# RetNet attention and a tanh-shrink feed-forward layer in one kernel: two thirds of the k and q transposes done by a DMA of 16-bit halves

**Chip, cores, metric.** One core of a Trainium2 chip. The metric is the device time of one execution in microseconds, the median of several. SBUF and PSUM are the core's on-chip memories (every tile here has up to 128 rows, called partitions), HBM is the memory outside the core.

## What the kernel computes

A recurrent attention block and, on its output, a feed-forward layer. All in float32.

```python
# attention: q, k, v of shape (4, 8, 768, 64), a state of 64x64 for each head
for t in range(S):
    state = gamma * state + k[:, :, t] (outer product) v[:, :, t]
    y[:, :, t] = scale * q[:, :, t] @ state
x = y.transpose(0, 2, 1, 3).reshape(B * S, H * D)      # 3072 x 512
# feed-forward: w_in 512 x 2048, w_out 2048 x 512
h = x @ w_in
out = (h - tanh(h)) @ w_out
```

## The kernel before

The kernel takes the sequence in 24 chunks of 128 tokens. A chunk's attention is a handful of small products on TensorE, in which k and q stand on the partitions by head dimension. So each chunk needs k and q transposed: four 128x128 blocks each. TensorE does it by matmuls with the identity, and ScalarE copies the result out of PSUM.

```python
def turn(ci, which, early=False):
    ...                                   # a pair of PSUM banks
    t = loaded[ci][which]
    for p in range(NP):                   # NP = 4 pairs of heads
        nc.tensor.transpose(tp[:, ts(p, P)],
                            t[:, ds(2 * p, 2)].rearrange("p h d -> p (h d)"), ident)

def turn_chunk(ci):
    if ci < NCH:
        turn(ci, 0)                       # k
        turn(ci, 1)                       # q
        turn_copy(ci)                     # one ScalarE copy, PSUM -> kqT in SBUF
```

Around the attention runs the feed-forward layer, as 96 steps. A step is an up projection (16 matmuls into h), the non-linearity (five activations on ScalarE, six operations on VectorE), and the down projection of two steps earlier (8 matmuls into o). The first 8 steps and the chunks 0 to 7 are ordered by hand. After that a loop feeds one chunk into every second step, and steps 8 to 26 also convert weight tiles, on ScalarE, VectorE and GpSimd (a cut; the conditions at both ends of the range are left out):

```python
with_chunk = {BEGUN + 2 * i + 1: FIRST - 3 + i for i in range(NCH - FIRST + 3)}   # 8, 8
for i in range(14, NW):
    with_weights[i - 5] = [i]

for s in range(BEGUN, len(steps)):
    ci = with_chunk.get(s)
    if ci is not None:
        scale(ci + 3, ...)                # GpSimd: q and v by powers of gamma
        outputs_rest(ci); keep_x(ci)
        products(ci + 2); mask(ci + 2); state(ci + 2)     # these need kqT of ci + 2
        load_chunk(ci + 4)
        outputs(ci + 1); see(ci + 1)
    for i in with_weights.get(s, []):
        convert(i); load_weights(i + 3)
    up(...); shrink(...)                  # (four calls)
    downs(LAG)                            # down of step s - 2; stores of results
    if ci is not None:
        turn_chunk(ci + 3)
```

All DMAs but one are issued on SyncE, whose queue is in program order: an entry that waits holds up those behind it.

## Time and profile before

| | before |
|---|---|
| median of 4 runs | 767.60 us (767.25 to 767.75) |
| span of the profiled run | 766.0 us |
| TensorE (PE) busy | 754.9 us, 99% |
| VectorE (DVE) busy | 524.5 us, 68% |
| ScalarE (ACT) busy | 375.3 us, 49% |
| DMA, mean of the span | 56 GB/s |

The lines on which the argument stands are shown in the prediction.

### The profile page before, as it was taken

Reading aid. Unit: us, or ns where it says so; the run is one execution under the profiler, and the core shown is the slowest. Engines: PE = TensorE matmul, PEld = TensorE weight load, DVE = VectorE, ACT = ScalarE, POOL = GpSimd, SP = SyncE. Lnnn points to the kernel's source line nnn. Section 1 sums busy time; section 2 is a strip of 40 time slices with the busy share of each in tenths; the row PEclk is TensorE's granted clock in tenths of the full one; section 3 lists DMA queues with packets and bytes.
Section 4 is the critical chain, followed back from the end, with each engine's and each line's share of the span. In section 5 each row is a group of like instructions: output and inputs, shape, how many; then the busy total and the mean of one; then the engine's idle time right before and its main releaser. Section 6 shows DMA issues by size and latency. Waiting matters only on the chain.

```text
span 766.0 us, 13968 instructions
## 1 busy us (share of the span) xinstructions
PE 754.9 (99%) x5598; PEld 517.1 (68%) x5598; DVE 524.5 (68%) x807; ACT 375.3 (49%) x709; POOL 124.3 (16%) x108
## 2 busy tenths in 40 slices
PE   8899999999999999999999999999999999999997
PEld 7776666677677667766766666666666666666663
DVE  4999899898898666556555665666655665666653
ACT  3666576565656444454443444434443444434442
POOL 0564444543443311110000000000000000000000
PEclk9999999999999999999999999999999999999999
DMA  9972444445441223320000000000000000000000
GB/s 204 225 188 57 125 111 111 124 115 121 113 110 43 69 70 77 97 50 2 15 15 1 14 15 0 29 0 1 27 1 1 27 1 0 29 0 1 27 1 27
DMA packets 89808, 42.99 MB, mean 56 GB/s; under 512 B 76304, under 2 KB 84624, under 8 KB 89744
## 3 DMA queue, kind: packets, MB, share of 16 engines
q1 hardware_dynamic: 89600, 41.95, 22.0%
q8 instruction: 44, 0.72, 0.4%
q10 hardware_dynamic: 144, 0.15, 0.1%
q14 instruction: 20, 0.16, 0.1%
HBM read 35.80 MB, written 6.29 MB: 55 GB/s over the span
## 4 chain that ended last, share of the span: by engine, by line
PE 95%; DVE 2%; SPq 1%; DMA 1%; ACT 0%; issue 0%; DVEq 0%
PE h L402 43%; PE o L450 42%; PE y L340 3%; PE kqTp L248 3%; PE s L286 1%; PE s L292 1%; SPq L227 1%; DMA raw<-in_moe_w_in_dram 1%; PE kqTp L210 0%; DVE head L183 0%; SPq L152 0%; DVE head L181 0%; PE y L210 0%; DVE power L185 0%; DVE head L179 0%
## 5 line engine op out<-in xcount | busy, mean ns | idle before, releaser
L402 PE MATMUL h<-xT,w 128*128 128x256 f32 x1536 | 349.9, 381 | 0.0
L450 PE MATMUL o<-w,g 128*128 128x512 f32 x768 | 345.5, 593 | 0.5 <-DVE g L441 0.5
L402 PEld LDWEIGHTS h<-xT,w 128*128 128x128 f32 x1536 | 288.5, 190 | 62.9 <-issue 26.5
L450 PEld LDWEIGHTS o<-w,g 128*128 128x128 f32 x768 | 145.5, 190 | 144.4 <-issue 136.3
L411 ACT ACTIVATE u<-h 128x512 f32<-128x512 f32 x96 | 57.3, 597 | 297.9 <-PE h L402 297.9
L427 DVE TENSOR_TENSOR th<-h,th 128x512 f32<-128x512 f32 x96 | 66.3, 691 | 183.9 <-ACT th L412 183.4
L441 DVE COPY_PREDICATED g<-large,th 128x512 f32<-128x512 int32 x96 | 75.4, 785 | 10.9 <-DVE g L440 1.4
L430 DVE SCALAR_TENSOR_TENSOR h<-q,h 128x512 f32<-128x512 f32 x96 | 66.9, 697 | 10.0
L436 DVE SCALAR_TENSOR_TENSOR h<-q,h 128x512 f32<-128x512 f32 x96 | 66.8, 696 | 9.9
L419 ACT ACTIVATE q<-u,tab 128x512 f32<-128x512 f32 x96 | 69.4, 723 | 0.0
L420 ACT ACTIVATE q<-u,tab 128x512 f32<-128x512 f32 x96 | 69.1, 720 | 0.0
L421 ACT ACTIVATE large<-u,tab 128x512 f32<-128x512 f32 x96 | 68.8, 717 | 0.0
L440 DVE TENSOR_TENSOR g<-h,u 128x512 f32<-128x512 f32 x96 | 66.3, 691 | 3.3
L428 DVE SCALAR_TENSOR_TENSOR h<-u,h 128x512 f32<-128x512 f32 x96 | 65.8, 685 | 0.0
L412 ACT ACTIVATE th<-h 128x512 f32<-128x512 f32 x96 | 56.8, 592 | 0.0
L193 POOL TENSOR_TENSOR low<-low,power 128x512 f32<-128x512 f32 x30 | 38.6, 1286 | 110.6 <-DVE power L185 55.0
L234 POOL TENSOR_TENSOR q<-q,tab 128x512 f32<-128x512 f32 x22 | 23.6, 1072 | 107.6 <-DMA q<-in_q_dram 101.9
L197 POOL TENSOR_TENSOR w<-low,head 128x512 f32<-128x512 f32 x30 | 38.5, 1283 | 2.4
L260 ACT COPY kqT<-kqTp 128x1024 f32<-128x1024 f32 x20 | 20.2, 1012 | 22.6 <-PE kqTp L248 22.4
L340 PEld LDWEIGHTS y<-a,v 64*64 64x64 f32 x768 | 16.1, 136 | 15.0 <-ACT large L421 11.4
L234 POOL TENSOR_TENSOR v<-v,tab 128x512 f32<-128x512 f32 x22 | 24.9, 1131 | 0.8 <-DMA v<-in_v_dram 0.8
L370 ACT COPY seen<-y 64x1 f32<-64x1 f32 x96 | 10.1, 154 | 24.8 <-PE y L340 24.4
(47 smaller groups left out, 398.1 us busy)
## 6 DMA issues: line engine op xcount, KB each, us to landing
k<-in_k_dram SPq DMA_DIRECT2D x24, 256.0 KB, 4.5
q<-in_q_dram SPq DMA_DIRECT2D x24, 256.0 KB, 5.0
v<-in_v_dram SPq DMA_DIRECT2D x24, 256.0 KB, 5.3
raw<-in_moe_w_out_dram SPq DMA_DIRECT2D x12, 512.0 KB, 3.5
out_dram<-sum SPq DMA_DIRECT2D x24, 256.0 KB, 2.0
raw<-in_moe_w_in_dram SPq DMA_DIRECT2D x14, 256.0 KB, 3.0
raw<-in_moe_w_in_dram SPq DMA_DIRECT2D x28, 128.0 KB, 3.5
raws<-in_moe_w_out_dram SPq DMA_DIRECT2D x4, 512.0 KB, 5.7
```

Of the source, the lines that this page charges most:

```text
L402: nc.tensor.matmul(hp, w1[:, c, ts(2 * m2 + i, P)], xT[n // 2][:, c, ts(n % 2, TH)], start=(i == 0 and c == 0), stop=(c == NC - 1), skip_g ...
L411: nc.scalar.activation(u, hp, AF.Square)
L419: nc.scalar.activation(q0, u, AF.Square, bias=bias0)
L420: nc.scalar.activation(q1, u, AF.Square, bias=bias1, scale=math.sqrt(A))
L421: nc.scalar.activation(large, u, AF.Relu, bias=bias_m)
L427: nc.vector.tensor_tensor(th, hp, th, op=ALU.subtract)
L428: nc.vector.scalar_tensor_tensor(hp, in0=u, scalar=R, in1=hp, op0=ALU.subtract, op1=ALU.mult, reverse0=True)
L430: nc.vector.scalar_tensor_tensor(hp, in0=q0, scalar=C0, in1=hp, op0=ALU.add, op1=ALU.mult)
L436: nc.vector.scalar_tensor_tensor(hp, in0=q1, scalar=A * C1, in1=hp, op0=ALU.add, op1=ALU.mult)
L440: nc.vector.tensor_tensor(flat, hp, u, op=ALU.mult)
L441: nc.vector.copy_predicated(flat, large.bitcast(I32), th)
L450: nc.tensor.matmul(o_p[j], gT[n, m2][:, i, ts(j, P)], w2[:, 2 * m2 + i], start=(first and i == 0), stop=(last and i == 1))
```

## The change

Its intent is to take the transposes of chunks 8 to 23 off TensorE. The transposing DMA is given 2-byte elements here (why is said in the prediction). So ScalarE separates the low and high 16 bits of k and q, a DMA stores the halves to a scratch in HBM as rows "token, half", and a transposing DMA loads them so that the two halves of a word lie side by side again in SBUF. As this way is long, a chunk comes in every third step only. Two small parts of the diff, a name for the 16-bit type and a default for a `pop`, are left out below.

```diff
+    dram = ctx.enter_context(tc.tile_pool(name="dram", bufs=2, space=bass.MemoryType.DRAM))
-    def turn_chunk(ci):
-        if ci < NCH:
-            turn(ci, 0)
-            turn(ci, 1)
-            turn_copy(ci)
+    def turn_by_dma(ci):
+        apart = mid.tile([P, 2, 2, H * D], U16, tag="apart", name=f"apart_{ci}", bufs=1)
+        for which in range(2):
+            words = loaded[ci][which].rearrange("p h d -> p (h d)").bitcast(U16)
+            nc.scalar.copy(out=apart[:, :, which],
+                           in_=words.rearrange("p (n two) -> p two n", two=2))
+        rows = dram.tile([P, 2, 2 * H * D], U16, tag="rows", name=f"rows_{ci}")
+        nc.sync.dma_start(out=rows, in_=apart.rearrange("p two i n -> p two (i n)"))
+        sides[ci] = mid.tile([P, 2, NP, P], F32, tag="kqT", name=f"kqT_{ci}")
+        nc.sync.dma_start_transpose(
+            out=sides[ci].rearrange("p i n t -> p (i n) t").bitcast(U16),
+            in_=rows.rearrange("p two n -> (p two) n"),
+        )
...
-    with_chunk = {BEGUN + 2 * i + 1: FIRST - 3 + i for i in range(NCH - FIRST + 3)}
+    with_chunk = {BEGUN + 3 * i + 1: FIRST - 3 + i for i in range(NCH - FIRST + 3)}
...
-        if ci is not None:
-            turn_chunk(ci + 3)
+        if ci is not None and ci + 3 < NCH:
+            turn_by_dma(ci + 3)
```

More of the change, by code (lines that the diff above doesn't have):

```diff
@@ L12 @@
 U32 = mybir.dt.uint32
+U16 = mybir.dt.uint16
 AF = mybir.ActivationFunctionType
@@ L327, in outputs @@
         vh = loaded[ci][2]
-        turned.pop(ci)
+        turned.pop(ci, None)
         qT = sides.pop(ci)[:, 1]
```

## The prediction

> **What bounds the kernel now.** I read the page from its first part to its fourth, and then the chain in order of time.
>
> ```profile
> span 766.0 us, 13968 instructions
> PE 754.9 (99%) x5598; PEld 517.1 (68%) x5598; DVE 524.5 (68%) x807; ACT 375.3 (49%) x709; POOL 124.3 (16%) x108
> PE 95%; DVE 2%; SPq 1%; DMA 1%; ACT 0%; issue 0%; DVEq 0%
> ```
>
> TensorE is busy for 99% of the span at a granted clock of 0.998, and 95% of the chain that ended last runs on it. A busy PE alone would not prove a bound. The chain in order of time does: it is the answer on one pair of steps, in which a chunk of the attention is fed into the stream of feed-forward tiles.
>
> ```profile
> 337.12 0.39 PE y L340 x16
> 337.52 0.47 PE s L286 x32
> 337.98 0.47 PE s L292 x32
> 338.45 0.70 PE y L340 x36
> 339.15 3.65 PE h L402 x16
> 342.80 3.43 PE o L450 x8
> 346.23 0.87 PE kqTp L248 x8
> 347.11 3.46 PE h L402 x16
> 350.56 1.72 PE o L450 x4
> ```
>
> The reader is to see that each piece begins where the one above it ended, and that the whole pair is on PE. The eight transposes of a chunk (kqTp) sit in this chain with 0.87 us. The last piece is cut by the window; the table of a wider window has it as 3.43 us. So a chunk costs PE 0.39 + 0.47 + 0.47 + 0.70 = 2.03 us for its products, 0.87 us for its transposes, and 3.65 - 3.46 = 0.19 us in the up projection after the products. A plain step is 3.46 + 3.43 = 6.89 us. The pair is 2.03 + 3.65 + 3.43 + 0.87 + 3.46 + 3.43 = 16.87 us, which is also the distance to the next pair in the trace. Nothing in it is a wait.
>
> **What the groups say of the operations concerned.** By form:
>
> ```profile
> L248 PE MATMUL kqTp<-tab,k 128*128 128x128 f32 x96 | 15.5, 287 | 0.3 <-DMA k<-in_k_dram 0.2
> L248 PE MATMUL kqTp<-tab,q 128*128 128x128 f32 x96 | 14.5, 274 | 0.0
> L260 ACT COPY kqT<-kqTp 128x1024 f32<-128x1024 f32 x20 | 20.2, 1012 | 22.6 <-PE kqTp L248 22.4
> L411 ACT ACTIVATE u<-h 128x512 f32<-128x512 f32 x96 | 57.3, 597 | 297.9 <-PE h L402 297.9
> L419 ACT ACTIVATE q<-u,tab 128x512 f32<-128x512 f32 x96 | 69.4, 723 | 0.0
> ```
>
> A transpose lasts some 280 ns by itself, but eight overlap to 0.87 us, that is 0.109 us each. The chain's number must be used: eight times the mean would give 2.2 us, and those are not to be had. ScalarE sits idle for 297.9 us waiting for PE, so it has room.
>
> **What the Trainium skill says.** Three places bear on this.
>
> "TensorE: Matmul & The Clock Gate", Part 4: PE-mode transpose: about 275 ns in a kernel's context, with the output in PSUM, so that a copy must follow. The trace agrees: 274 and 287 ns, and the copy is the group of 1012 ns.
>
> "DMA: Bandwidth & Descriptors", DMA Transpose (X-bar): only 2-byte elements, only into SBUF. Hence the halves: ACT splits low and high words, and their transposes interleave again into 32-bit words. The same page, Latency and other measured facts, gives the DMA transpose 261 GB/s in one kernel. No run before has one, so the trace cannot confirm it.
>
> "VectorE: DVE Perf Modes", The three transpose paths: 1309 ns for one 128x128 block of 16-bit elements by DMA. The trace is silent on this too. A chunk has 2 (k, q) x 4 x 2 (halves) = 16 such blocks. Whether they run side by side or in a row is the main uncertainty here.
>
> **The change part by part.**
>
> Removed from PE: the transposes of chunks 8 to 23, 16 chunks of 0.873 us (from pairs of this chain with 0.87 and 0.88) = 14.0 us. They are all on the path. The up projection after them takes 3.46 us, as it does after a down projection, so no further gain hides there. The PSUM pair used for them becomes free, but no PE wait was for it in the steady part.
>
> Moved: a chunk comes every three steps instead of two. Its work is the same. The last one comes at step 8 + 3*18 + 1 = 63 instead of 45. Tile column n=11, which needs chunks 22 and 23, begins at step 88, and n=4, which needs chunks 8 and 9, begins at step 32 and gets the latter at step 21. So the slower pace costs nothing by itself, and the new period is 16.87 - 0.87 + 6.89 = 22.89 us.
>
> Added on ScalarE: two copies of 1024 elements of a partition each, SBUF to SBUF, in place of one from PSUM. A 512-wide operation takes 0.72 us from SBUF (L419) and 0.60 from PSUM (L411), so I estimate 1.01 + 0.12 = 1.13 us each, 2.26 us for a chunk. That is 1.25 us more, 20 us in all, beside PE.
>
> Added on the queues: a store of 512 KB to HBM, a wait on the same queue until it has landed, and a transposing load of 512 KB. What landing takes today:
>
> ```profile
> k<-in_k_dram SPq DMA_DIRECT2D x24, 256.0 KB, 4.5
> v<-in_v_dram SPq DMA_DIRECT2D x24, 256.0 KB, 5.3
> raw<-in_moe_w_out_dram SPq DMA_DIRECT2D x12, 512.0 KB, 3.5
> out_dram<-sum SPq DMA_DIRECT2D x24, 256.0 KB, 2.0
> ```
>
> The store lies between the 2.0 us of half as much and the 3.5 us of a load of the same size; I take 3.0, and 0.2 for the issue.
>
> Is it in time? I measure from the beginning of a chunk's step (337.12 in the chain). These rows of ScalarE's timeline show the moment at which it is free:
>
> ```profile
> 345.03 0.71 ACT L421 ACTIVATE large<-u,tab 128x512 f32<-128x512 f32 x1
> 347.14 1.01 ACT L260 COPY kqT<-kqTp 128x1024 f32<-128x1024 f32 x1 [1.40 <-PE kqTp L248]
> ```
>
> At 345.74, so 8.62 us in, the step's activations end, and the new copies can begin at once (q was scaled by GpSimd long before, since its chunk was loaded a period earlier). Copies end at 8.62 + 2.26 = 10.88; the store has landed at 10.88 + 3.2 = 14.1. The products that need the result begin one period later, after the products of k and v: 22.89 + (337.98 - 337.12) = 23.75. The transposing load may therefore take 23.75 - 14.1 = 9.6 us from issue to landing before PE waits at all.
>
> What will it take? 512 KB at the skill's 261 GB/s is 2.0 us, and some 2 to 3 us go to issue and receipt, as for the other transfers, so 4 to 5 us. The loads of k, q and v support this: they move 768 KB in 256-byte pieces and all have landed some 6.5 us after the first issue (two issues of about 0.5 us, then 5.3). My estimate is 5 us (4 to 7), which leaves 4 to 5 us to spare. Sum: 767.5 - 14.0 = 753.5 us. I add 0.7 us for occasional late weights or stores on the same in-order queue: **754.2 us**, a gain of 1.7%.
>
> **The rivals.**
>
> A: a wait takes the place of the work. If the 16 blocks run one after the other, the load takes 16 x 1.309 = 20.9 us, PE waits 20.9 - 9.6 = 11.3 us for each chunk, and the time is 753.5 + 16 x 11.3 = 934 us. A milder form, 12 us to landing, gives 2.4 us each and 792 us. For it: the number in the skill, and that the pace was slowed to three steps, which says that the way through HBM is long. Against it: other transfers of this shape spread over all 16 engines. At two steps the room would be 9.6 - 6.9 = 2.7 us, too little even for my 5 us, so the third step is explained without this rival.
>
> B: the issuing queue becomes the bound. SyncE now stands still until the store has landed, and weights and stores of results queue behind it. For it: until about step 28 it carries a weight tile a step. Against it: the weights are asked for three steps ahead, and the stall is some 3 us in 22.9. I expect 0 to 3 us in all, or 754 to 757.
>
> C: ScalarE delays the stream. It has 2.26 us more after the activations, and the next step's h is ready only at 9.11 + 3.46 = 12.57 us, against copies that end at 10.88. It stays hidden; if the halves were twice as slow as estimated (4.5 us, ending at 13.1), the next activations slip by half a microsecond, which the lag of two tiles absorbs. 753.5.
>
> D: more gain than counted. It would need over 15.4 us from PE to pass 2%, and only 14.0 are there.
>
> **Range and chances.** The mechanism without waits ends between 752 and 757 us; I give that some 70%. Some 10% go to small waits, up to 775. The rest, 20%, is a transposing load that is well over its 9.6 us, with no natural upper end. So the range is 751.5 to 775. To be over 2% faster, the time must be under 752.2, which the sum barely forbids: 5%. To be over 2% slower it must be over 782.9, rival A: 18%. Within 2%: 77%.
>
> **What would show each step right or wrong.** Right: the L248 groups fall from 96 to 32 each, the chain in order of time holds products, up, down, up, down, up, down without a gap in 22.89 us, PE busy falls by some 14 us, the two ACT copies take about 1.1 us, and the issue table shows the store at about 3 and the transposing load at 4 to 7 us. Wrong: a wait of PE or PEld at the products (s) for a DMA into kqT, or a landing time above 9.6 us; then rival A holds, and the time lost should be 16 times the excess. Waits of the weight conversion for its DMA would be rival B, and PE waits for ACT or DVE in a chunk's steps rival C.

## More of the kernel before

One more view is of use later: the busy share in 40 equal slices of the span (19 us each; 9 is 90% or more).

```profile
PE   8899999999999999999999999999999999999997
DVE  4999899898898666556555665666655665666653
```

PE is full from the third slice on. DVE, whose mean is 68%, is nearly full up to the thirteenth slice, some 250 us: this is where the weights are converted. A mean over the span hides that.

## The result

| | before | after |
|---|---|---|
| median | 767.60 us | 754.76 us (754.43 to 754.93, 4 runs) |
| span of the profiled run | 766.0 us | 752.6 us |
| PE busy | 754.9 us | 739.6 us |
| ACT busy | 375.3 us | 389.1 us |
| DMA, mean | 56 GB/s | 79 GB/s |

The ratio is 0.9833 (95% interval 0.9816 to 0.985), that is 12.8 us or 1.7% faster. Ratios here are the mean time of one kernel's fast runs over that of the other's of the same rounds, so not quite the ratio of the medians quoted.

From the page of the changed kernel, the span, the engines, and the two new kinds of transfer with their median time to landing:

```profile
span 752.6 us, 13801 instructions
PE 739.6 (98%) x5470; PEld 501.9 (67%) x5470; DVE 518.7 (69%) x807; ACT 389.1 (52%) x725; POOL 125.9 (17%) x108
rows<-apart SPq DMA_DIRECT2D x16, 512.0 KB, 2.6
kqT<-rows SPq DMA_TRANSPOSE x16, 4.3
```

PE has 5470 matmuls in place of 5598: 128 less, 16 chunks of 8. Its busy time fell by 15.3 us where 14 were forecast; 1.1 of these lie in the first 97 us (90.81 against 89.75), before the loop. The store lands in 2.6 us (predicted 3.0), the transposing load in 4.3 us (predicted 5). The groups by form (line, engine, operation, shapes, count | busy us, mean ns | idle before):

```profile
L250 PE MATMUL kqTp<-tab,k 128*128 128x128 f32 x32 | 5.1, 282 | 0.4 <-DMA k<-in_k_dram 0.3
L250 PE MATMUL kqTp<-tab,q 128*128 128x128 f32 x32 | 5.0, 278 | 0.2 <-DVE q L236 0.2
L273 ACT COPY apart<-q 128x1024 uint16<-128x1024 uint16 x16 | 16.8, 1048 | 0.0
L273 ACT COPY apart<-k 128x1024 uint16<-128x1024 uint16 x16 | 16.6, 1036 | 0.0
```

Transposes on PE fell from 96 to 32 of each kind. The two copies of 16-bit words take 1.04 us each (estimated 1.13). The chain that ended last, in order of time, over one period:

```profile
353.48 0.39 PE y L352 x16
353.87 0.47 PE s L298 x32
354.34 0.47 PE s L304 x32
354.81 0.70 PE y L352 x47
355.51 3.65 PE h L414 x16
359.16 3.43 PE o L462 x8
362.59 3.45 PE h L414 x16
...
372.93 3.43 PE o L462 x8
376.37 0.39 PE y L352 x16
```

There is no gap: the period is 376.37 - 353.48 = 22.89 us, as worked out ahead. The products that read kqT (s L304) begin as soon as those before them end, so the load is in time.

Where did the 14.0 us go that the transposes had taken? I compared the start of the first up matmul of each step in the two traces. At step 9, before the first chunk of the loop, the changed kernel is 0.50 us ahead (104.11 against 104.60), from the hand-ordered beginning, whose waits made it end up to 1.3 us earlier or later in the traces taken here. At step 64, after the last chunk, it is 13.39 us ahead. So the loop won 12.9 us, 1.1 less than 14.0. The loss is at one place. Step 15 begins 9.89 us after step 14 where 8.77 are usual, since PE waited for DVE (timeline of the changed kernel, rows of DVE and PE):

```profile
142.95 0.73 DVE L453 COPY_PREDICATED g<-large,th 128x512 f32<-128x512 int32 x1
143.57 1.28 DVE L471 TENSOR_TENSOR sum<-o,sum 128x512 f32<-128x512 f32 x2
...
144.30 1.12 PE L462 MATMUL o<-w,g 128*128 128x512 f32 x2 [0.86 <-DVE sum L471]
```

The down projection needs a PSUM bank that DVE has yet to add to the running sum. DVE runs without a pause there (from 118 to 147 us in its timeline).

### The profile page after: what moved, and what is told of

Its sections match the earlier page's. It is cut to its first block, busy times and chain, and to the rows that moved or that the text cites. A ratio compares the mean times of both kernels' runs of the same rounds, so it can differ in the third digit from the quotient of the medians.

```text
span 752.6 us, 13801 instructions
## 1 busy us (share of the span) xinstructions
PE 739.6 (98%) x5470; PEld 501.9 (67%) x5470; DVE 518.7 (69%) x807; ACT 389.1 (52%) x725; POOL 125.9 (17%) x108
## 4 chain that ended last, share of the span: by engine, by line
PE 94%; DVE 2%; DMA 1%; SPq 1%; ACT 1%; issue 1%; DVEq 0%; ACTq 0%
PE h L414 43%; PE o L462 43%; PE y L352 3%; PE s L298 2%; PE s L304 1%; DMA raws<-in_moe_w_in_dram 1%; PE kqTp L250 1%; DMA k<-in_k_dram 1%; SPq L229 1%; PE kqTp L212 0%; DVE head L185 0%; PE y L212 0%; SPq L154 0%; DVE head L183 0%; DVE g L453 0%
## 5 line engine op out<-in xcount | busy, mean ns | idle before, releaser
L453 DVE COPY_PREDICATED g<-large,th 128x512 f32<-128x512 int32 x96 | 72.1, 751 | 10.6 <-ACT apart L273 0.5
L236 POOL TENSOR_TENSOR v<-v,tab 128x512 f32<-128x512 f32 x22 | 26.5, 1206 | 0.2 <-DMA v<-in_v_dram 0.2
L352 PE MATMUL y<-a,v 64*64 64x64 f32 x768 | 21.1, 224 | 2.3 <-issue 1.8
```

The costliest lines, as they stand in the source:

```text
L352: nc.tensor.matmul(y[ds(D * col, D), r, p // 2, ts(a, D)], lhsT, rhs, start=start, stop=True, skip_group_check=True)
L453: nc.vector.copy_predicated(flat, large.bitcast(I32), th)
```

## The experiments

My theory: the gain is TensorE's time for the 128 transposes and nothing else; the way through HBM is free because it has time to spare; the missing 1.1 us is DVE's backlog. The rivals: that the slower pace, or the freed PSUM banks and ScalarE's copy, made part of the gain; that the load only just comes in time; that something other than DVE ate the 1.1 us.

### The pace alone (e1), and both ways at once (e6)

```diff
 e1, on the kernel before:
-    with_chunk = {BEGUN + 2 * i + 1: ...
+    with_chunk = {BEGUN + 3 * i + 1: ...
 e6, on the changed kernel:
         if ci is not None and ci + 3 < NCH:
+            turn(ci + 3, 0)
+            turn(ci + 3, 1)
             turn_by_dma(ci + 3)
```

> The kernel before with only the pace changed: a chunk every three steps, all transposes still on TensorE. Theory (the whole gain is TensorE's time for 128 transposes, the pace is worth nothing): 767.6 us, within 1.5 us. Rival (the slower pace itself relieves ACT, DVE or GpSimd in the steps that convert weights, and part of the gain comes from it): 755 to 764 us.

> The changed kernel with the 128 transposes put back on TensorE, their results unused; the halves still go through HBM and their result is what is used. Theory (TensorE's time alone makes the gain, and the way through HBM costs nothing): 128 x 0.109 = 14.0 us more, less the 1.1 us for which TensorE waited on DVE anyway, so 767.6 to 768.8 us. Rival (the gain came from the PSUM pair and from ACT's copy out of PSUM being gone, or the DMAs slow TensorE): under 764 or over 771 us.

Measured: e1 768.1 us (ratio to before 1.0004, 0.9989 to 1.0019), e6 767.81 us (1.0002, 0.9987 to 1.0017). The pace by itself is worth nothing. With the transposes back on TensorE, unused, the gain is gone, although the DMAs, the copies and the free time of ScalarE are as in the changed kernel. The traces show it without the scatter of the beginning: from the start of step 9 to that of step 95, the last, the kernel before takes 643.02 us, e1 643.03, e6 643.03, and the changed kernel 630.12. In e6 step 15 begins the usual 8.77 us after step 14: with PE slower, DVE keeps up. So the transposes cost 767.81 - 754.76 (of an earlier call) = 13.05 us, and with the 1.1 us of waiting that they replace 14.2 us, 0.111 us each, against 0.109 read from the chain. Both expectations held.

### Half of the change (e11)

```diff
-        for which in range(2):
-            words = loaded[ci][which].rearrange("p h d -> p (h d)").bitcast(U16)
+        words = loaded[ci][1].rearrange("p h d -> p (h d)").bitcast(U16)
...                                        # apart and rows half as large
-            out=sides[ci].rearrange("p i n t -> p (i n) t").bitcast(U16),
+            out=sides[ci][:, 1].bitcast(U16),
...
+        turn(ci, 0)
+        nc.scalar.copy(out=sides[ci][:, 0],
+                       in_=turned[ci][:, 0].rearrange("p (n t) -> p n t", n=NP))
```

> Half of the change: q of chunks 8 to 23 by the DMA, k transposed on TensorE. Theory (each transpose taken off TensorE is worth 0.109 us): 64 are back, 7.0 us, less the up to 1.1 us of waiting for DVE, so 760.6 to 762 us. The load is half as large; if its landing time is a fixed part plus bytes, 2.5 to 3.5 us, if it is all fixed, 4.3. Rival (gain in proportion to something else, say the PSUM pair or ACT's copy out of PSUM, which this variant keeps): 765 us or more.

Measured: 760.74 us (0.9907), in the expected range. Against 754.69 us of the changed kernel that is 6.05 us for 64 transposes, and no wait of PE for DVE's sum is left in its trace, so 6.05 + 1.1 = 7.15 us, 0.112 us each. This variant keeps the PSUM pair and a ScalarE copy out of it, so those were not the source of the gain. The issues of its page:

```profile
rows<-apart SPq DMA_DIRECT2D x16, 256.0 KB, 2.0
kqT<-rows SPq DMA_TRANSPOSE x16, 3.3
```

256 KB land in 3.3 us, 512 KB in 4.3. By these two medians the load is some 2.3 us plus 1.0 us for each 256 KB.

### How much room there is: two and three loads (e4, e8, e5), a faster and a slower pace (e2, e9, e3)

The room can be measured by lengthening the way or by shortening the period. First the doubled load and the pace of before:

```diff
 e4, on the changed kernel:
+        for _ in range(2):
             nc.sync.dma_start_transpose(...)
 e2, on the changed kernel:
-    with_chunk = {BEGUN + 3 * i + 1: ...
+    with_chunk = {BEGUN + 2 * i + 1: ...
```

> The changed kernel with the transposing load issued twice into the same tile, the second after the first has landed. Theory (6.1 us of room are left, and a second load needs 4.3 to 4.6): no wait, 754 to 756 us. Rival (the load just about arrives in time, or its traffic costs TensorE something): over 758 us, up to 825 us if all 4.4 us of 16 chunks show.

> The changed kernel at the pace of before, a chunk every two steps. Theory: the way from the beginning of a chunk's step to the landed result takes 8.6 + 2.0 (copies) + 2.7 (store) + 4.3 (transposing load) = 17.6 us, and the products come at 16.0 + 0.86 = 16.86 us, so TensorE waits some 0.75 us for each of 16 chunks: 764 to 770 us, and the wait shows at the products of kqT. Rival 1 (the room was larger than thought, the third step was needless): 753 to 756 us. Rival 2 (the queue jams with loads and weights, waits of several us): over 775 us.

Both missed, each towards the rival that had named a higher time. e4 took 758.1 to 760.3 us in its three fast runs (mean 759.1; 0.9887); a fourth, 971.2 us at a clock of 0.753 from beginning to end, is left out, as is its profile. e2 took 797.51 us (1.0379). The lists of waits of e2 confirm where:

```profile
PE s L304 <- DMA kqT<-rows: 29.2, 16, 5.6
```

All 16 chunks wait, but 29.2 us is not 16 x 0.75. By chunk, the pause of PE ahead of the products (here and below from start to start, some 0.2 us more each than in the list of waits) was 0.7 to 1.2 us in ten of them, as expected, 2.2 and 3.7 us in chunks 9 and 8, and 3.6 to 5.8 us in chunks 17 to 20. For one of these, chunk 19, the issuing queue of e2 shows why:

```profile
317.94 0.95 SPq L478 DMA_DIRECT2D out_dram<-sum  x2
318.99 0.41 SPq L276 DMA_DIRECT2D rows<-apart  x1
322.03 2.55 SPq L278 DMA_TRANSPOSE kqT<-rows  x1
```

The copies had ended at 316.55, but the store to the scratch was issued at 318.99: two stores of results stood ahead of it and waited for DVE's sum. The changed kernel has the same at chunks 14 and 16. For chunk 14 its copies ended at 249.57:

```profile
250.97 0.95 SPq L478 DMA_DIRECT2D out_dram<-sum  x2
252.01 1.72 SPq L276 DMA_DIRECT2D rows<-apart  x1
256.75 1.76 SPq L278 DMA_TRANSPOSE kqT<-rows  x1
```

From the issue of the load to the products there are then 5.9 us in chunk 14 and 7.6 in chunks 8 and 16, and 9.6 to 10.9 in the others. So one load (4.3 us) is in time everywhere, and two (8.7 us) are too late by 2.8 + 1.1 + 1.1 = 5.0 us, close to e4's loss of 759.1 - 754.8 = 4.3 us (an estimate, as e4's own trace is of the slow state). This explanation was then tested by issuing the store and the loads of a chunk ahead of the stores of results:

```diff
 in e8 (two loads), e9 (pace of two steps) and e5 (three loads):
+        if ci is not None and ci + 3 < NCH:
+            turn_by_dma(ci + 3)
         downs(LAG)
-        if ci is not None and ci + 3 < NCH:
-            turn_by_dma(ci + 3)
```

> The kernel with two transposing loads in a row, with the store and the loads issued ahead of the stores of results of the same step. Theory (the 4.8 us lost by the doubled load came from chunks 14 and 16, whose store to the scratch waited for stores of results in the same in-order queue, and from chunk 8): only chunk 8 still waits, 754.5 to 757 us. Rival (a second load costs everywhere, by traffic or by being too late in most chunks): 758.5 us or more, as without the reordering.

> Pace of two steps, store and load issued ahead of the stores of results. Theory (the 797 us had two parts: 0.7 to 1.2 us of waiting in each chunk, and in chunks 17 to 20 a further 3 to 5 us for the queue's order, with the lower clock that followed such gaps): gaps of 0.7 to 1.2 us in all chunks but 8 and 9, 770 to 780 us. Rival (the long gaps come from the traffic itself): 790 us or more.

> Pace of three steps, three transposing loads in a row, issued ahead of the stores of results. Theory (room of 10.3 us from the first issue to the products, against 4.4 + 4.4 + 4.3 = 13.1 us): a gap of 2.8 us in each of 16 chunks, 45 us, so 795 to 810 us. Rival (loads in a row overlap or are quicker than one alone): under 780 us.

Measured: e8 755.42 us (0.9841), with no pause but one of 0.9 us at chunk 8; room is 10.3 us in chunks 14 and 16 too. Its steps 9 to 95 take 630.15 us, those of the changed kernel 630.12: the pause at chunk 8 takes the place of most of the wait for DVE at step 15. e9 773.78 us (1.0076), with pauses of 0.7 to 1.1 us in 15 chunks and 3.7 us at chunk 8. Both as expected: a second load of 512 KB a chunk is free, and the room ends between two loads and three, as it ends between a period of three steps and of two.

e5, with three loads, took 833.57 us (1.0854), slower than the 795 to 810 expected. The direction is right, the size is not. The pauses come to 51.3 us in the list of waits, 3.2 us a chunk, since some loads took up to 6 us. The rest is the clock, the share of TensorE's full clock that was granted. Two stretches of e5, one before and one after a pause of PE (columns: window, length, busy us of PE, PEld, DVE, ACT and POOL with counts, granted clock, DMA share, GB/s):

```profile
400.00:405.00 5.00, 5.00 (x45) 2.68 (x47) 2.48 (x4) 3.38 (x6) 0.00 (x0) 1.00 0.53 120
409.00:412.00 3.00, 3.00 (x8) 2.38 (x8) 0.59 (x2) 0.26 (x3) 0.00 (x0) 0.50 0.67 153
```

The granted clock is 1.00 before and 0.50 after, and the up projection that follows took 5.2 us instead of 3.56 (start to start). In e5 the up projection was slow, over 4.0 us, in 13 of 16 chunks, and the trace's record of the clock has 13 falls to 0.50 there, of 3.4 or 6.8 us each; in e2 it was so in the five chunks that paused for 3.6 us or more. So a pause of some us costs up to 2.5 us more than itself in the up projection, and with the small products before it up to 3 us. It adds up: against the changed kernel the pauses of e5 delay the products by 54 us, the slower matmuls after them take 27 us more, and the 1.1 us of waiting for DVE is gone, 80 us in all; from step 9 to step 95 e5 takes 80.4 us more.

Last, more room than needed:

```diff
 e3, on the changed kernel:
-    with_chunk = {BEGUN + 3 * i + 1: ...
+    with_chunk = {BEGUN + 4 * i + 1: ...
```

> The changed kernel at a pace of four steps. Theory (pace is worth nothing as long as the load lands in time): 754 to 756 us. Rival (the work of chunks, spread wider, meets DVE's backlog or the last tiles differently): more than 1.5 us from the changed kernel.

Measured: 755.07 us (0.9833), as expected, against 754.69 of the changed kernel. A fourth step wins nothing.

### The missing 1.1 us (e7, e10, and e12 for comparison)

```diff
 e7, on the changed kernel:
     for i in range(14, NW):
-        with_weights[i - 5] = [i]
+        with_weights.setdefault(i - 4 if 16 <= i < 24 else i - 5, []).append(i)
 e10: the same with 16 <= i < 21, and the order of e8
 e12: the changed kernel as it is
```

> The changed kernel with the conversion of eight weight tiles (16 to 23) begun one step later. Theory (the 1.1 us that are missing from the 14.0 are TensorE waiting for DVE, which carries a backlog of weight conversion up to step 15): the wait of TensorE for DVE's sum goes, 753.4 to 754.2 us, about 1 us under the changed kernel. Rival (the missing 1.1 us is something else, or the backlog only moves): 754.5 to 756 us, with the wait still there or at another step.

> The changed kernel with the store and the load of a chunk issued ahead of the stores of results, and only weight tiles 16 to 20 converted one step later (22 and 23, which made the last try late, stay where they are). Theory (moving DVE's work off the steps before 15, without making a weight late, gives back the missing 1.1 us): 753.3 to 754.3 us, about 1 us under the changed kernel of the same call, no wait of TensorE for DVE's sum. Rival (every move of the conversions makes another wait): the same as the changed kernel or over it.

> The changed kernel once more, for comparison in the same call: 754.5 to 755.5 us.

Measured: e7 757.23 us (0.9862), e10 755.83 us (0.9844), e12 754.69 us (0.9828). In e7 and e10 the wait at step 15 is gone: it begins 8.77 us after step 14 in both. But each has a new one. In e7's list of waits:

```profile
PE o L462 <- POOL w L199: 2.8, 1, 2.8
```

I had delayed tile 23 into the very step that needs it, and tile 22 to the step before, a mistake of the edit. That step took 11.56 us instead of 6.89, 4.7 more, as the clock fell to 0.50 for 3.4 us after the pause. In e10, which leaves those where they were, DVE's work comes back six steps later:

```profile
PE o L462 <- DVE sum L471: 1.4, 1, 1.4
```

There step 21 begins 10.66 us after step 20 instead of 9.01. e10's hand-ordered beginning was also 1.3 us later at step 9 than e12's, for no cause that I looked into, so its total says less than its steps: from step 9 to 95 it takes 0.5 us more than the changed kernel. Shown is that the wait at step 15 belongs to DVE's work in the steps before it, for it vanishes with eight conversions moved and nothing else changed (e7), with five moved and the order of e8 (e10), and with PE made slower (e6). The expectation that a move would give the 1.1 us back failed twice: the rival of e10, that the wait moves, is what happened. No version here beats the changed kernel.

## Why the prediction was right

The time was predicted as 754.2 us and is 754.76. The mechanism was right; that the numbers are within 0.6 us is in part luck, as the last point says.

- **What bounds it, and the price of a transpose.** Right. PE's chain was the place to read it: 0.873 us for eight was confirmed by adding 128 back (14.2 us with the replaced wait), and 64 (7.15 us). The mean of a single transpose, 280 ns, would have promised over twice as much.
- **The pace costs and gives nothing.** Right by e1 and e3.
- **ScalarE's added copies are hidden.** Right: 1.04 us each, no wait of PE for them.
- **The room.** I had 9.6 us for the load; the trace shows some 10.3 in a usual chunk, since store and copies were quicker, and 5.9 in the worst. The worst case was not foreseen: that the in-order queue puts two stores of results ahead of the scratch store in some chunks. It cost nothing with one load of 4.3 us, and e4 and e8 show that it would have with a slower one.
- **The load's time.** Estimated at 5 us, measured 4.3. Rival A, blocks in a row for 20.9 us, is refuted by the same number.
- **The 0.7 us added for late weights or stores.** The size is near (1.1 us lost, 0.5 won in the beginning) by luck, for the cause is another. No weight and no store was late. PE waited for DVE, which is near its own limit up to some 250 us, and I had looked at its mean of 68% only. My rival C reckoned with ScalarE, and only its sign named DVE too; it should have asked about VectorE in the steps that convert weights.

## What to carry to other kernels

When an engine is full from end to end, work taken off it is worth its share of the chain in order of time, not its count times the mean duration, and only up to the next engine's limit in that stretch: look at the busy share by slice, not at the mean. A detour by DMA was free here as long as the period left it room; work out that room from the moments at which the inputs are ready and the result is used, for the chunk in which the issuing queue is fullest. Where the room is short, issue the urgent transfers ahead of stores that wait for other engines, and add to a pause of the matmul engine of some 2 us or more the lower clock that may follow it, here up to 3 us more.

## What the Trainium skill lacked or had wrong

- "DMA: Bandwidth & Descriptors", Latency and other measured facts: its 261 GB/s for a DMA transpose agrees with the slope measured here (1.0 us for a further 256 KB, 262 GB/s; from two medians rounded to 0.1 us), but alone it gives 2.0 us for 512 KB where 4.3 were measured. The page has a fixed part of about 2.0 us, but for DMAs issued from GpSimd, and gives none for this kind; by the two sizes run here it is some 2.3 us.
- "VectorE: DVE Perf Modes", The three transpose paths: 1309 ns for a 128x128 block by DMA is not a price for each block. Sixteen blocks in one DMA landed in 4.3 us, 0.27 us a block. The table does not say so; only the note below it, which gives this path some 90% of the DMA bandwidth, points that way.
- "TensorE: Matmul & The Clock Gate", Part 1: it puts the fall to half clock at an idle window of about 3.4 us. All pauses over 3.0 us in e2, e5 and e9 were followed by a slow up projection here, but so were three of the five pauses of 2.1 to 2.6 us in e5, next to small products that keep TensorE only partly busy. In e7 a pause of 2.8 us between full-size matmuls was followed by a clock of 0.50 for 3.4 us too.
